# A block table that is worked out earlier: attention and a routed expert layer in one kernel

## The chip, the cores and the metric

The kernel runs on one core of a Trainium2 chip. The metric is the device time of one execution in microseconds (us); for the kernel before, the median of 3 runs is 975.67 us (975.44 to 978.47).

## The reference, cut to what matters

64 attention heads of 576 tokens and 64 dimensions (8 batches of 8 heads), with scores far below the row's largest left out, and then a layer of 8 experts in which each of the 4608 tokens goes to the one expert with the largest logit:

```python
scores = scale * q @ k.T                       # per head, 576 x 576
attn   = softmax(scores where scores >= max(scores) - tau)
x      = (attn @ v) laid out as 4608 x 512     # the 8 heads of a token side by side
logits = x @ w_gate                            # 4608 x 8
for e in range(8):                             # expert_idx = argmax(logits)
    xe = x[expert_idx == e]
    out[expert_idx == e] = gate_w * (relu(xe @ w1[e]) @ w2[e])
```

## The kernel before, in words

The attention half works on 32 pairs of heads, four pairs to a batch `b`. A counter `k` of steps runs through it, 11 steps to a pair. In each step the program emits one tile of scores (`s`, for the row maxima, ahead of the rest by 21 steps), one tile of transposed scores (`st`), its exponential and mask, the casts `ph` and `pl` of the result, and some of the products with v (`av`). All else is hung on steps: `plan(k, f)` and `after(d, f)` have `f` emitted in step `k` or `d` steps from now, at the front, the middle or the end of a step.

Emission order is not yet queue order. When the program is complete, a planner walks a simulated time line and fills each engine's queue: of the instructions that it reckons ready, the one emitted first goes first. An instruction whose inputs and buffers are there early can so be placed far ahead of its step. Each queue then runs strictly in its order, and so do the DMA issues on the queues of SP, ACT and POOL.

When the four pairs of a batch are through, `finish(b)` (L510) normalizes the batch's tokens and writes them into the rows `R`; SP transposes them (`xTg`, L552); `logits(b)` (L560) multiplies with the gate; `route(b)` (L585) finds each token's expert. Nine steps after `route` for batch 5, `ranks` (L616) counts with matmuls (`rk`) which place every token has in its expert's list, writes the places to `posi` (L630), and `send(j)` (L643) lets POOL scatter five tiles of rows to `xs` in DRAM, in steps 6, 8, 10, 12 and 14 after the ranks.

Behind the last scatters of the batches 5, 6 and 7 comes a block table each: `tables0`, `tables1`, `tables2` (L1047 to L1062, named in the dictionary `TABLES`, L1100). `level` calls `counts` (L672: one matmul into a PSUM tile `pc`) and `table_first` (L679): a chain of 11 small VectorE operations and one ScalarE copy, most of them on `pc` itself, that ends in the integer tables `badi` and `row` (both by L669). From `row`, `fetch(m)` (L830) lets POOL gather 128 rows of block `m` out of `xs` (`Rm`, L858); the gather waits for the scatters of the batches placed so far. SP transposes the rows (`xTm`, L868), VectorE and POOL copy their weights and numbers (`gt`, L871 and L876). From step 336 on the products with the experts' weights (`gemm1`, L913, and `gemm2`, L946) run beside the last attention steps, and after step 352 alone.

PSUM: the tiles `pst`, `lg`, `rk` and `pc` share one buffer, the pool `ps_m` with a single bank, so one of them is there at a time. `pst` (L381) is a pair's row maxima, transposed on TensorE; four small operations (L386 to L389) turn them into three rows `ptT`, and three DMAs of SP (L394) put these into the operand `CQ`, which the pair's `st` matmuls (L407) read. The steps are: ranks of batch 5 in step 311, `pst` of pair 30 in 320, `pst` of pair 31 in 331, logits of batch 6 in 335.

Between these steps, too, the first expert's weights are brought in, eight pieces through two buffers `wf`: SP loads a piece (L802), ScalarE casts it (`wb`, L817), TensorE copies the cast to PSUM (`hi_w`, L254), VectorE takes the difference (L255) and frees the buffer.

Of the kernel before, what the change touches and what calls it, by code (L numbers as in the profile page):

```python
# [18 lines left out]
B, H, S, D = 8, 8, 576, 64  # L19
# [31 lines left out]
def kernel(  # L51
# [123 lines left out]
    def plan(k, f, where=END):  # L175
        if urgent[0]:
            f = hurry(f)
        assert (k, where) >= (now[0], slot[0])
        acts.setdefault(k, ([], [], []))[where].append(f)
# [11 lines left out]
    def after(k, f, where=END):  # L191
        plan(now[0] + k, f, where)
# [392 lines left out]
    def route(b, n, dist, Lj, w, got):  # L585

        bc = [P, n, E]

        def t3(nm, dt=F32):
            return small.tile([P, 5, E], dt, tag=nm, name=f"{nm}_{b}", bufs=2)[:, 0:n, :]  # L590

        def t2(nm, dt=F32):
            return small.tile([P, 5, 1], dt, tag=nm, name=f"{nm}_{b}", bufs=2)[:, 0:n, :]

        tt = nc.vector.tensor_tensor
        mx, mw, oh, ex, sm = t2("mx"), t2("mw"), t3("oh", F16), t3("ex"), t2("sm")
        was = small.tile([P, E], F16, tag="was", name=f"was_{b}", bufs=2)
        posi = small.tile([P, 5], I32, tag="posi", name=f"posi_{b}", bufs=2)
        R = rows_of(b)
        Rf = R.bitcast(F32)  # L600
        chain(0, [
            lambda: nc.vector.tensor_reduce(mx, Lj, axis=AX.X, op=ALU.max),
            lambda: tt(w, Lj, mx.to_broadcast(bc), ALU.is_equal),
            lambda: tt(ex, Lj, mx.to_broadcast(bc), ALU.subtract),
            lambda: tt(w, w, rank8.unsqueeze(1).to_broadcast(bc), ALU.mult),
            lambda: nc.vector.tensor_reduce(mw, w, axis=AX.X, op=ALU.max),
            lambda: tt(oh, w, mw.to_broadcast(bc), ALU.is_equal),
            lambda: nc.scalar.copy(was, run),
            lambda: nc.vector.tensor_reduce(got, oh.rearrange("p j e -> p e j"), axis=AX.X, op=ALU.add),
            lambda: nc.scalar.copy(  # L610
                R[:, 0:n, DM + 1:DM + 2], tid[:, b // 2, 4 * (b % 2):4 * (b % 2) + n].unsqueeze(2)
            ),
            lambda: tt(run, run, got, ALU.add),
        ], b == B - 1)

        def ranks(dist=dist):  # L616
            nc.scalar.activation(ex, ex, AF.Exp, scale=1.0 / (SX * SG))
            rk = ps_m.tile([P, 512], F32, tag="m", name=f"rk_{b}")
            rkv = rk[:, 0:n * E].rearrange("p (j e) -> p j e", e=E)
            for j in range(n):  # L620
                nc.tensor.matmul(rkv[:, j], before, oh[:, j], start=True, stop=False)
                for i in range(j):
                    nc.tensor.matmul(rkv[:, j], ones, oh[:, i], start=False, stop=False)
                nc.tensor.matmul(rkv[:, j], ones, was, start=False, stop=True)
            ps = rk[:, 64:64 + n * E].rearrange("p (j e) -> p j e", e=E)
            total = rk[:, 136:136 + n].unsqueeze(2)
            after(1, lambda: tt(ps, rkv, oh, ALU.mult), FRONT)
            def places():
                with nc.allow_low_precision(reason="one whole number below 2^24 among zeros"):
                    nc.vector.tensor_reduce(posi[:, 0:n].unsqueeze(2), ps, axis=AX.X, op=ALU.add)  # L630

            fs = [
                lambda: nc.vector.tensor_reduce(total, ex, axis=AX.X, op=ALU.add),
                lambda: nc.scalar.activation(sm, total, AF.Copy, bias=1e-9),
                places,
                lambda: nc.vector.reciprocal(sm, sm),
                lambda: nc.scalar.activation(Rf[:, 0:n, DM:DM + 1], sm, AF.Copy, scale=1.0 / (SX * SW * SW)),
            ]
            if b == 0:
                fs.append(lambda: nc.vector.tensor_copy(pos0, posi[:, 0:1]))  # L640
            chain(1, fs, b == B - 1)

            def send(j):  # L643
                put = nc.gpsimd.indirect_dma_start(
                    xs[:, :], bass.IndirectOffsetOnAxis(ap=posi[:, j:j + 1].bitcast(U32), axis=0), R[:, j, :], None
                )
                if b < B - 1:
                    tc.keep_in_program_order(put)
                put = put.ins
                tc.declare_no_dep(put, group="puts", reason="each token has a row of its own")  # L650
                tc.declare_no_dep(put, group="gets", reason="gathered rows are those of tokens placed earlier")
                tc.add_to_no_dep_group("puts", put)
                puts.append((b, put))
                sent.add((b, j))

            wait = 1 if b == B - 1 else 6
            if b == B - 1:
                dist = 0
            for j in range(n):
                after(wait + dist * j, lambda j=j: send(j))  # L660
            if b in TABLES:
                after(wait + dist * n, TABLES[b])

        after(0 if b == B - 1 else RK[b], ranks)


# [160 lines left out]
    def late(m):  # L827
        return m == "x" or m >= NEARLY

    def fetch(m):  # L830

        idx, bad, par = slots[m]
        g, i = group_of[m] if m != "x" else ((m,), 0)
        if m in range(NF, NF + 2):

            if "spare" not in T:
                T["spare"] = xp.tile([P, 2, NT * H * W // 2], F32, tag="x", name="spare")
            Rm = T["spare"][:, m - NF, 0:ROW].bitcast(I32)
            xT = T["spare"][:, m - NF, 520:1032].bitcast(F16).rearrange("p (i c t) -> p i c t", i=1, c=8)
        elif m in range(EARLY_SLOTS):  # L840
            Rm = pools[0].tile([P, ROW], I32, tag="Rm", name=f"Rm_{m}", bufs=2)
            xT = pools[0].tile([P, 1, 8, P], F16, tag="xTm", name=f"xTm_{m}", bufs=NF)
        else:
            Rm = R[:, 0 if m == "x" else m % 5]
            if i == 0:
                xT = rpool.tile([P, 2, 8, P], F16, tag="xT", name=f"xTm_{m}", bufs=3)
            else:
                xT = ms[g]["xT"]
        if i == 0:
            ms[g] = dict(xT=xT, par=par, gw=[], ti=[])  # L850
        d = ms[g]
        for z in range(1 + late(m)):
            dst = xT[:, i]
            if late(m):
                Rm = R[:, z if m == "x" else (2 * m + z) % 5]
                dst = xT.rearrange("p i c t -> p (i c t)")[:, 0:8 * PL].rearrange("p (c t) -> p c t", c=8)
                d["xT"], dst = dst, dst[:, :, P * z:P + P2 * z]
            get = nc.gpsimd.indirect_dma_start(  # L858
                Rm, None, xs[:, :], bass.IndirectOffsetOnAxis(ap=idx[:, z:z + 1].bitcast(U32), axis=0)
            )  # L860
            get = get.ins
            mine = [put for b, put in puts if b <= placed.get(m, B - 1)]
            for put in mine:
                tc.add_manual_dep(get, put.name, sync, reason="rows of the tokens placed so far")
            if m != "x":
                tc.declare_no_dep(get, group="puts", keep=mine, reason="rows of tokens placed later are others")
                tc.add_to_no_dep_group("gets", get)
            nc.sync.dma_start_transpose(dst, Rm[0:P2 if z else P, 0:DM].bitcast(F16))  # L868
            gt = small.tile([P, 2], I32, tag="gt", name=f"gt_{m}_{z}", bufs=6)
            gw, ti = gt.bitcast(F32)[:, 0:1], gt[:, 1:2]  # L870
            nc.vector.tensor_copy(gw, Rm.bitcast(F32)[:, DM:DM + 1])  # L871
            to = Rm[:, DM + 1:DM + 2]
            if z:
                nc.gpsimd.tensor_tensor(ti, to, to, ALU.add)
                to = ti
            nc.gpsimd.tensor_tensor(ti, to, bad[:, z:z + 1], ALU.add)  # L876
            d["gw"].append(gw)
            d["ti"].append(ti)
# [168 lines left out]
    def tables0():  # L1047
        T[0] = level("0", ((), EARLY[0]), None)
        for m in range(NF):
            after(1 + m, lambda m=m: fetch(m))  # L1050

    def tables1():
        T[1] = level("1", EARLY, T[0])
# [46 lines left out]
    TABLES = {B - 3: tables0, B - 2: tables1, B - 1: tables2}  # L1100
# [5 lines left out]
    wait = []  # L1106
# [64 lines left out]
    if True:  # L1171
# [18 lines left out]
        while busy:  # L1190
# [3 lines left out]
            for z in (("st", "s"), ("s", "st"))[TUNE["ord"]]:  # L1194
                n, t = divmod(k + (NSTEP + LEAD if z == "s" else 0), NSTEP)
# [11 lines left out]
            n, t = divmod(k - TUNE["av"], NSTEP)  # L1207
# [95 lines left out]
```

## Time and profile before

| what | value |
|---|---|
| median of 3 runs | 975.67 us |
| the profiled execution | 985.67 us, span 983.8 us |
| PE busy | 940.2 us (96%) |
| DVE busy | 696.7 us (71%) |
| ACT busy | 652.0 us (66%) |
| POOL busy | 555.4 us (56%) |
| granted TensorE clock, mean | 0.990 |

PE is TensorE's matmuls, PEld its weight loads, DVE VectorE, ACT ScalarE, POOL GpSimd; a q behind a name is the engine's own instruction queue, with its DMA issues. A time line row has the start, the duration, the line, out<-in, and in brackets how long the engine stood idle before and what ended it. `x2` behind a row means two such instructions merged into one row. Attention alone fills the span up to some 550 us; both halves share it until 563.5 us, where the last `st` matmul stands; after it the experts run alone.

### The profile page before, as it was taken

To read this page: it belongs to the slowest core of one execution; us is meant where nothing else is said; L and a number is where in the kernel's file an instruction comes from. 1 tells how busy PE (TensorE), PEld (TensorE's weight loads), DVE (VectorE), ACT (ScalarE), POOL (GpSimd) and SP (SyncE) were. 2 spreads that over 40 slices of the span, in tenths; PEclk is the share of its full clock that TensorE was granted. 3 is DMA by queue.
4 is the path that set the end of the run, shared out by engine and by line. 5 is a ranking of instruction groups with operands and counts; after the bars stand their busy time and mean duration, and the time that the engine had idled before them with its cause. 6 is when DMAs were issued, how large, how long until landed. Compare 5 with 4: busy or idle time off the path is not lost. (4 is left out here: it accounts for less than half of the span.)

```text
span 983.8 us, 28575 instructions
## 1 busy us (share of the span) xinstructions
PE 940.2 (96%) x11548; PEld 604.5 (61%) x11548; DVE 696.7 (71%) x1413; ACT 652.0 (66%) x1111; POOL 555.4 (56%) x467
## 2 busy tenths in 40 slices
PE   7899999999999999999997989999999999999997
PEld 2355556556566566555564676677667766677684
DVE  8899999999999999999889755735143342433560
ACT  2789898989988989989788844434243342433651
POOL 5466886997978988879879743331212221221121
PEclk9999999999999999999999999999999999999999
DMA  7643455474645664645647469987574556556630
GB/s 199 186 133 77 137 135 146 92 197 115 162 121 166 153 165 107 175 129 119 141 132 196 92 157 306 383 210 190 156 242 123 198 162 170 182 150 217 214 107 28
DMA packets 142707, 159.19 MB, mean 162 GB/s; under 512 B 96361, under 2 KB 112747, under 8 KB 142572
## 3 DMA queue, kind: packets, MB, share of 16 engines
q1 hardware_dynamic: 125782, 100.03, 40.2%
q10 hardware_dynamic: 7638, 27.85, 9.2%
q0 software_dynamic: 9152, 29.45, 8.7%
q8 instruction: 92, 1.51, 0.6%
q14 instruction: 43, 0.35, 0.1%
HBM read 90.24 MB, written 19.44 MB: 111 GB/s over the span
## 5 line engine op out<-in xcount | busy, mean ns | idle before, releaser
L432 POOL TENSOR_TENSOR pl<-e,ph 128x1024 f16<-128x1024 f32 x158 | 336.0, 2137 | 95.2 <-ACT ph L431 56.2
L423 ACT ACTIVATE e<-st,ntau 128x512 f32<-128x512 f32 (+1 forms) x352 | 222.0, 652 | 52.9 <-PE st L407 40.8
L426 DVE SCALAR_TENSOR_TENSOR e<-st,e 128x512 f32<-128x512 f32 (+1 forms) x352 | 219.4, 636 | 12.6 <-ACT e L423 12.0
L946 PE MATMUL y<-wb,hl 128*128 128x512 f16 (+1 forms) x1056 | 203.5, 362 | 0.5 <-ACT xh L491 0.4
L913 PEld LDWEIGHTS <-wb 128*128 128x128 f16 x2304 | 188.3, 98 | 24.6 <-issue 5.2
L913 PE MATMUL h<-xTm,wb 128*128 128x256 f16 (+2 forms) x2112 | 196.3, 253 | 3.0 <-issue 2.5
L370 DVE TENSOR_REDUCE nm<-s 128x1 f32<-128x512 f32 x300 | 188.3, 632 | 14.2 <-PE s L360 12.6
L476 PE MATMUL av<-vop,ph 128*128 128x65 f16 (+3 forms) x3072 | 188.9, 195 | 1.7 <-ACT x L486 1.2
L476 PEld LDWEIGHTS <-ph 128*128 128x128 f16 (+1 forms) x3072 | 158.7, 100 | 47.1 <-issue 17.5
L431 ACT CAST ph<-e 128x1024 f16<-128x1024 f32 x160 | 166.6, 1042 | 5.2 <-DVE e L426 4.6
L476 PE MATMUL av<-vop,pl 128*128 128x65 f16 (+1 forms) x1536 | 168.0, 194 | 1.3 <-POOL pl L432 0.7
L476 PEld LDWEIGHTS <-pl 128*128 128x128 f16 (+1 forms) x1536 | 136.2, 100 | 32.4 <-issue 9.9
L946 PEld LDWEIGHTS <-hl 128*128 128x128 f16 (+1 forms) x1056 | 94.5, 100 | 100.0 <-issue 5.0
L407 PE MATMUL st<-CQ,ck 128*128 128x512 f16 (+3 forms) x640 | 137.4, 289 | 4.1 <-DMA CQ<-ptT 4.1
L825 DVE SCALAR_TENSOR_TENSOR wb<-wf,wb 128x1024 f16<-128x1024 f32 x88 | 103.9, 1221 | 52.4 <-ACT wb L817 50.5
L406 PE MATMUL st<-QK 128*128 128x512 f16 (+3 forms) x640 | 138.9, 294 | 1.5 <-DVE e L426 0.6
L358 PE MATMUL s<-QK 128*128 128x512 f16 (+1 forms) x600 | 129.0, 292 | 1.0 <-DVE nm L370 0.3
L960 POOL DMA_INDIRECT out_dram<-o,gt x40 | 44.8, 1119 | 145.7 <-ACT o L957 129.4
L360 PE MATMUL s<-ck,CQ 128*128 128x512 f16 (+1 forms) x600 | 126.9, 287 | 0.0
L901 ACT ACTIVATE hl<-h 128x512 f16<-128x512 f32 (+1 forms) x80 | 45.8, 573 | 111.7 <-PE h L913 103.0
L817 ACT ACTIVATE wb<-wf 128x1024 f16<-128x1024 f32 x96 | 97.5, 1049 | 30.8 <-DMA wf<-in_w_dram 16.0
L957 ACT ACTIVATE o<-y,gt 128x512 f32<-128x512 f32 (+1 forms) x40 | 26.6, 664 | 93.7 <-PE y L946 76.6
(193 smaller groups left out, 981.6 us busy)
## 6 DMA issues: line engine op xcount, KB each, us to landing
wf<-in_w_dram SPq DMA_DIRECT2D x96, 512.0 KB
qkf<-in_qk_dram ACTq DMA_DIRECT2D x29, 576.0 KB
vf<-in_v_dram ACTq DMA_DIRECT2D x15, 640.0 KB
QK<-hi SPq DMA_DIRECT2D x62, 144.0 KB
QK<-lo SPq DMA_DIRECT2D x62, 72.0 KB
QK<-hi SPq DMA_DIRECT2D x62, 72.0 KB
ck<-lo SPq DMA_DIRECT2D x62, 72.0 KB
CQ<-hi SPq DMA_DIRECT2D x62, 64.0 KB
```

The source lines that it names most:

```text
L358: nc.tensor.matmul(sc[rows, oc], d["QA"][a][:, cols], d["KB"][a][:, CH[c]], start=True, stop=False)
L360: nc.tensor.matmul(sc[rows, oc], d["CQ"][:, at:at + cols.stop - cols.start], d["CK"][a][:, CH[c]], start=False, stop=True,)
L370: nc.vector.tensor_reduce(o, sc[:, 0:width(t)], axis=AX.X, op=ALU.max, negate=True)
L406: nc.tensor.matmul(sc[rows, oc], d["KB"][a][:, cols], d["QA"][a][:, CH[c]], start=True, stop=False)
L407: nc.tensor.matmul(sc[rows, oc], d["CK"][a][:, cols], d["CQ"][:, q], start=False, stop=True)
L423: nc.scalar.activation(pf, sc, AF.Exp, bias=ntau, scale=0.125 / SS)
L426: nc.vector.scalar_tensor_tensor(pf, sc, 0.0, pf, ALU.is_ge, ALU.mult)
L431: nc.scalar.copy(h, pd)
L432: (nc.vector if (n, t) in PLV else nc.gpsimd).tensor_tensor(l, pd, h, ALU.subtract)
L476: nc.tensor.matmul(av[:, 0:D] if z == 2 else av, l if z == 1 else h, vop[:, tv, W:W + D] if z == 2 else vop[:, tv, 0:W], start=i in (0, NT ...
L913: nc.tensor.matmul(o, Wt[:, c, wh, f], x, start=c == 0 and z == 0, stop=c == 3 and z == 2,)
L946: nc.tensor.matmul(o, h[:, hh], Wt[:, f, wh, c], start=f == 0 and z == 0, stop=f == 7 and z == 2)
```

## The change

In `ranks`, the table of batch 5 is emitted 5 steps after the ranks and not 6 + 2 x 5 = 16 steps after them. `tables0` has its three fetches 12, 13 and 14 steps after itself and not 1, 2 and 3, so that they are emitted in the steps 328 to 330 as before. The two other tables are as they were.

```diff
@@ -659,7 +659,7 @@
             if b in TABLES:
-                after(wait + dist * n, TABLES[b])
+                after(5 if b == B - 3 else wait + dist * n, TABLES[b])
@@ -1047,7 +1047,7 @@
     def tables0():
         T[0] = level("0", ((), EARLY[0]), None)
         for m in range(NF):
-            after(1 + m, lambda m=m: fetch(m))
+            after(12 + m, lambda m=m: fetch(m))
```

The table's step so goes from 327 to 316: ahead of the five scatters (steps 317 to 325) and of `pst` of pair 30 (step 320).

## Rows read from the trace of the kernel before

**Rows 1.** The page, busy times: engine, busy us, share of the span, instructions.
```profile
PE 940.2 (96%) x11548; PEld 604.5 (61%) x11548; DVE 696.7 (71%) x1413; ACT 652.0 (66%) x1111; POOL 555.4 (56%) x467
```
**Rows 2.** Stretches: us, length, busy of PE PEld DVE ACT POOL, clock, DMA share, GB/s.
```profile
509.00:521.00 12.00, 10.59 (x149) 5.97 (x150) 9.50 (x22) 11.26 (x23) 9.74 (x8) 1.00 0.53 176
510.00:550.00 40.00, 32.52 (x484) 19.33 (x481) 32.36 (x72) 34.23 (x62) 35.20 (x27) 0.96 0.64 178
535.00:539.00 4.00, 3.59 (x35) 1.92 (x35) 2.83 (x8) 3.65 (x7) 3.81 (x3) 0.58 0.45 139
```
**Rows 3.** Waits of PE from 480 to 640 us: total us, times, longest.
```profile
PE hi_w L254 <- ACT wb L817: 3.9, 3, 2.0
```
**Rows 4.** Time line of PE.
```profile
514.05 0.27 PE L381 MATMUL pst<-ident,r 128*9 128x128 f32 x1
...
530.65 0.59 PE L254 MATMUL hi_w<-wb,ident_h 128*128 128x512 f16 x2 [1.50 <-ACT wb L817]
...
532.89 0.38 PE L407 MATMUL st<-CQ,ck 128*128 128x512 f16 x1
...
535.41 1.01 PE L254 MATMUL hi_w<-wb,ident_h 128*128 128x512 f16 x2 [1.96 <-ACT wb L817]
...
541.77 0.28 PE L381 MATMUL pst<-ident,r 128*9 128x128 f32 x1
...
551.49 0.38 PE L407 MATMUL st<-CQ,ck 128*128 128x512 f16 x1
...
552.75 1.07 PE L913 MATMUL h<-xTm,wb 128*128 128x128 f16 x16 [0.45 <-DMA xTm<-Rm]
```
**Rows 5.** Line 685: duration ns min/median/max, first and last start.
```profile
L685 DVE CAST rk_f<-rk_i x1: 172/172/172, 18.1 to 18.1; 128x32 f32<-128x32 int32 x1
```
**Rows 6.** Instructions on tile pc alone, 523 to 542 us: busy of PE DVE ACT.
```profile
523.00:542.00 19.00, 0.17 (x1) 2.10 (x11) 0.18 (x1) 0.91 0.80 214
```
**Rows 7.** Time line of DVE, first table and what stands around it.
```profile
508.93 0.18 DVE L630 TENSOR_REDUCE posi<-rk 128x5 int32<-128x40 f32 x1
...
522.77 0.27 DVE L389 TENSOR_TENSOR ptT<-pst,ptT 9x128 f16<-9x128 f32 x1
...
523.69 0.14 DVE L676 TENSOR_TENSOR cnt<-pc,base_e 128x8 f32<-128x8 f32 x1
...
541.53 0.19 DVE L669 CAST row<-pc 128x32 int32<-128x32 f32 x1
```
**Rows 8.** Time line of DVE, first and last operation of the second table.
```profile
569.48 0.17 DVE L676 TENSOR_TENSOR cnt<-pc,base_e 128x8 f32<-128x8 f32 x1 [2.42 <-PE pc L674]
...
573.15 0.19 DVE L669 CAST row<-pc 128x32 int32<-128x32 f32 x1
```
**Rows 9.** Time line of ACT.
```profile
516.42 0.36 ACT L386 ACTIVATE ptT<-pst,thr 9x128 f16<-9x128 f32 x1 [0.27 <-PE st L407]
...
575.33 0.20 ACT L610 COPY R<-tid 128x5 int32<-128x5 int32 x1 [0.95 <-DMA xs<-R,posi]
```
**Rows 10.** DMA issues on the queue of SP, in order of time.
```profile
520.87 2.89 SPq L394 DMA_DIRECT2D CQ<-ptT  x2
...
542.53 6.16 SPq L394 DMA_DIRECT2D CQ<-ptT  x3
548.74 1.26 SPq L868 DMA_TRANSPOSE xTm<-Rm  x1
```
**Rows 11.** Time line of POOL.
```profile
529.08 0.99 POOL L644 DMA_INDIRECT xs<-R,posi  x1 [0.17 <-issue]
...
532.37 4.21 POOL L432 TENSOR_TENSOR pl<-e,ph 128x1024 f16<-128x1024 f32 x2
...
544.04 1.01 POOL L858 DMA_INDIRECT Rm<-xs,row  x1 [0.15 <-DVE vop L255]
...
572.29 0.99 POOL L644 DMA_INDIRECT xs<-R,posi  x1 [0.17 <-issue]
```
**Rows 12.** Waits of SP's queue from 480 to 600 us.
```profile
SPq L868 <- DMA Rm<-xs,row: 4.7, 1, 4.7
```

## The prediction

> **What bounds the kernel now.** The busy times of the page come first: PE is busy 940.2 of 983.8 us [rows 1], so a change elsewhere counts only where it lengthens or shortens an idle stretch of PE. The busy times by stretch show where the change falls: from 510 to 550 us PE is busy 32.52 of 40 us [rows 2], so 7.5 us are idle there, the most that a better order can win besides the clock. The waits of PE name their cause: 3.9 us in three waits for ScalarE's cast of a weight piece [rows 3], the two longest 1.50 and 1.96 us, at 530.65 and 535.41 us [rows 4]. After the second one the matmuls are slower (two of 512 columns take 1.01 us, after the first wait 0.59) [rows 4]; the granted clock from 535 to 539 us is 0.58 on the mean [rows 2], between its levels of 1.2 and 2.4 GHz, which costs 0.42 x 4 = 1.7 us. The table itself comes from the time lines: it has the bank of `pst` from 523.7 us (its first VectorE operation) to 541.7 us (the end of `row`), 18.0 us [rows 7], for 11 VectorE operations of 2.10 us, one of ScalarE of 0.18 and a matmul of 0.17 [rows 6]. No wait of PE there is for the table or for a `pst` that it kept out. One row more says how much a step is worth: the table's constant, which the program emits in step 327, was converted at 18.1 us [rows 5]. The planner takes what is ready; a step is a rank, not a time.
>
> **Part by part, in the profiled execution's time.**
>
> *The table's operations* are moved, none is added. The bank is free from 509.1 us on, when `posi` of the ranks is written [rows 7], and step 316 comes about then, so I put its start at 509 to 511 us. Its 2.10 us on VectorE then fall into 509 to 521 us, where VectorE is busy 9.50 of 12 us [rows 2] and so has 2.5 us free: 0. Without that cover they cost at most their 2.1 us; from 523 to 542 us they leave 2.1 us free, at best a gain of as much.
>
> *How long the table keeps the bank.* Between 4.1 us (the second table, from 569.48 us to the end of its `row` at 573.34 us, plus 0.2 for its matmul) [rows 8] and 18.0 us [rows 7]: its end lies between 513.2 and 527.1 us. At step 316 its links are older than nearly all else that is ready, so it is nearer to the second table; with one large VectorE operation slipped into each gap, 11 x (0.19 + 0.68) = 9.6 us. I take its end at 515 to 519 us.
>
> *`pst` of pair 30* is now behind the table, a new wait. It is on PE at 514.05 us [rows 4], so it comes 1 to 5 us later. Behind it stand ScalarE's operation at 516.42 us [rows 9], VectorE's last at 522.77 us [rows 7], and SP's last row DMAs, issued until 520.87 + 2.89 = 523.8 us [rows 10]. The four small operations sum to about 1.2 us; from 514.3 to 523.0 us they have 8.7. So a `pst` 5 us late can still be done by 523 us. The first reader is the matmul at 532.89 us [rows 4], 9.1 us behind the last issue. Cost 0. At the other end (table until 527.1 us, 13 us late) the issues end at 536.8 us, a landing of 2.05 us (a scatter issued until 573.28 us is waited for until 575.33 [rows 9, 11]) makes it 538.9 us, and PE waits 6.0 us.
>
> *`pst` of pair 31* loses its wait: it ran at 541.77 us, right behind `row` [rows 4, 7]. It can come up to 3.6 us earlier, and the logits of batch 6 behind it. Its reader at 551.49 us does not wait [rows 4], though SP's last issue ends only at 542.53 + 6.16 = 548.7 us [rows 10]. Gain 0, but a spare of 2.8 - 2.05 = 0.75 us gets wider.
>
> *Gathers, `xTm`, `gt`.* Their steps are kept, their time is not: they were held up to 544.04 us [rows 11] by `row`. Now the last scatter decides, issued until 530.07 us and landed 2.05 us later at 532.1 us; then POOL has two `pl` until 536.6 us [rows 11]. So two gathers come some 7.5 us earlier, on POOL ahead of later `pl`, which shift by 2 x 1.3 us and win that back where the gathers stood: 0 (uncovered 2.6). Their transposes move up on SP, in front of the rows of pair 31, perhaps: 0 in the forecast, a rival below. The first expert matmul waited 0.45 us for `xTm` [rows 4]; that goes: -0.45. The next input in question is the weight piece, which is there before.
>
> *The fetches' distance and ScalarE's copy* move 0.
>
> Sum: -0.45 us on 985.67 us. That execution is 10.0 us above the median of 975.67 us; I carry the difference over to the median: 975.2 us. About 0.3% (2.9 us) is what a measurement here can tell from no change, so this is no change.
>
> **The rivals.**
>
> A, faster: the weight pieces get through sooner. The table's links stand between VectorE's differences that free `wf`, in a stretch in which PE waits for the pieces [rows 3]. If their 2.1 us leave that loop, half of the 3.9 us of waits goes (1.95), the stretch of lower clock goes with it (1.7), and the 0.45 above: -4.1 us, 971.6 us. For it: PE idles 7.5 us there [rows 2]. Against it: the last step before the waits is a DMA and a cast, and a link takes only 0.19 us of VectorE.
>
> B, slower: SP's queue. The transposes of the blocks come to stand ahead of SP's three row DMAs of pair 31 and hold them while they wait for the gather; such a wait is 4.7 us in this trace [rows 12]. The last row then is issued at 548.7 + 4.7 = 553.4 and landed at 555.4 us, and the matmul at 551.49 us waits 3.9 us. Of the two longest waits for weights one was followed by the low clock [rows 4], so half of 1.7 us comes on top: +4.8 us, 980.4 us. It decides from a delay of 0.75 us on, the spare worked out above. For it: steps 328 to 330 rank ahead of 334, that of the rows; in the kernel before the three transposes begin at 548.74 us, right behind the rows [rows 10]. Against it: the planner counts a gather's landing before it takes its transpose, and `pst` of pair 31 has moved up as well.
>
> The trace so shows the low clock after one of two waits. The Trainium skill, "TensorE: Matmul & The Clock Gate", section "HAM oscillation — how this bites in real kernels", describes it as paid at every wait for a DMA between short bursts. By that rule B has the whole 1.7 us and ends at 3.9 + 1.7 = 5.6, at 981.3 us; the trace disagrees at 530.65 us, and I keep the half.
>
> C, the change does not do what it says: the planner starts the table late again, behind `pst` of pair 30, since it goes by readiness. Then all stays, 975.7 us. Against it: `pc` ranks ahead of this `pst` now, and the bank is free before the pair's maxima are there.
>
> **How the numbers follow.** Forecast 0.47, C 0.05, A 0.27, B 0.21. A's size is at the bound of 2.9 us if only its waits or only its clock come, so a fifth of it falls within; what the new order does to the rest of the queues can push the forecast out on either side, a little over 0.1 together. So faster 0.28, within 0.3% 0.49, slower 0.23. The range goes from A with a little more (970.5) to B with the whole clock term (981.0); the forecast's own is 973 to 978. The 6.0 us of the late `pst` lie just outside.
>
> **What would show it.** Right: in the changed kernel's time line the first table lies between 509 and 520 us; `pst` of pair 30 comes up to 5 us later and its reader does not wait; `pst` of pair 31 stands nearer to 538 than 541.8 us; the first gathers stand at 535 to 538 us; PE is idle 7 to 8 us from 510 to 550 us as before. A shows in fewer waits for `wb` and a clock near 1.00 there; B in a wait of the `st` matmul for `CQ` or a longer one for `wb`, with transposes of blocks ahead of them on SP. The prediction is wrong if the time leaves 973 to 978 us, or if the gathers stay at 544 us.

## The result, and the profile after

The changed kernel takes 986.21 us (median of 5 runs, 982.63 to 987.09), the kernel before in the same set 975.98 us (975.44 to 978.47): a ratio of 1.0082, 95% interval 1.0063 to 1.0100. It is slower by 0.8%, where no change was forecast. Every ratio to the kernel before leaves out slow runs (one only, of the kernel before in the last set, at 999.23 us) and is not the quotient of two medians, which would be 1.0105 here. The level of the kernel before differs between the sets that follow, and drifts within them (medians from 978.11 to 990.27 us), so times are compared within a set.

The profiled execution of the changed kernel is the shortest of its five, 982.63 us with a span of 980.9 us, and that of the kernel before was 10 us above its median: the two traces can't be subtracted as they are. The changed one is 4.2 us ahead already when `posi` is written (504.71 against 508.93 us), before either table begins, so I count from there where times of the two are compared. From `posi` to the last `st` matmul (L407) it needs 57.2 us, the kernel before 54.6, and 55.0 in a second trace. So the first trace shows where time is lost, but only 2.2 to 2.6 us of it. Traces of the changed kernel in the second and fourth set need 63.1 and 61.3 us there; none of the kernel before was taken beside them. The stretch to look at is the one in which the table now lies. Busy times (length, busy of PE, PEld, DVE, ACT, POOL, then clock, DMA share, GB/s) that answer to [rows 2]:

```profile
510.00:550.00 40.00, 29.85 (x412) 17.36 (x410) 30.73 (x71) 31.29 (x55) 33.81 (x29) 0.87 0.72 179
...
520.00:525.00 5.00, 1.91 (x19) 1.25 (x19) 1.91 (x4) 2.67 (x10) 4.81 (x5) 0.52 0.16 58
525.00:530.00 5.00, 4.98 (x21) 1.99 (x20) 4.07 (x8) 3.39 (x5) 4.17 (x5) 0.79 1.06 221
```

PE is idle 10.2 of these 40 us, not 7.5, and its clock is 0.87, not 0.96. The worst five microseconds of the forty begin at 520 us: PE and DVE are busy 1.9 of 5 us each, ACT 2.7. Where three engines idle at once they may be waiting for each other in a row, and the time lines tell in which order. PE's, with the copies of weight pieces 3, 4, 5 and 7 (compare [rows 4]):

```profile
519.57 0.28 PE L381 MATMUL pst<-ident,r 128*9 128x128 f32 x1 [1.35 <-DVE row L669]
523.09 1.01 PE L254 MATMUL hi_w<-wb,ident_h 128*128 128x512 f16 x2 [3.25 <-ACT wb L817]
527.47 0.59 PE L254 MATMUL hi_w<-wb,ident_h 128*128 128x512 f16 x2
532.29 0.59 PE L254 MATMUL hi_w<-wb,ident_h 128*128 128x512 f16 x2 [2.31 <-DVE nm L370]
...
537.59 0.27 PE L381 MATMUL pst<-ident,r 128*9 128x128 f32 x1
540.72 1.01 PE L254 MATMUL hi_w<-wb,ident_h 128*128 128x512 f16 x2 [2.36 <-ACT wb L817]
...
589.12 0.48 PE L570 MATMUL lg<-wg,xTg 128*128 128x8 f16 x12 [3.47 <-DMA xTg<-R]
```

PE stands at `pst` of pair 30 until the table's `row` is written, and right behind it, 3.25 us more, at the copy of the third weight piece. The table (compare [rows 7]; it has the bank from its matmul at 506.3 us) and ScalarE around `pst` (compare [rows 9]):

```profile
504.71 0.18 DVE L630 TENSOR_REDUCE posi<-rk 128x5 int32<-128x40 f32 x1
...
507.41 0.16 DVE L676 TENSOR_TENSOR cnt<-pc,base_e 128x8 f32<-128x8 f32 x1
...
519.32 0.19 DVE L669 CAST row<-pc 128x32 int32<-128x32 f32 x1
521.45 0.35 DVE L387 SCALAR_TENSOR_TENSOR pst<-pst,thr,ptT 9x128 f32<-9x128 f32 x1 [1.94 <-ACT ptT L386]
```
```profile
519.12 1.06 ACT L817 ACTIVATE wb<-wf 128x1024 f16<-128x1024 f32 x1
...
521.06 0.36 ACT L386 ACTIVATE ptT<-pst,thr 9x128 f16<-9x128 f32 x1
521.83 0.25 ACT L388 CAST ptT<-pst 9x128 f16<-9x128 f32 x1 [0.41 <-DVE pst L387]
521.99 1.05 ACT L817 ACTIVATE wb<-wf 128x1024 f16<-128x1024 f32 x1
```

The copy at 523.09 us starts 0.05 us behind the end of the cast at 521.99 us. That cast had no wait for its data (no bracket names a DMA); it stood behind L388, the third small operation on `pst`. So the row is: `row`, `pst` on PE, L386, L387, L388, the cast, the copy. SP stands still too. Its queue (compare [rows 10]):

```profile
504.30 10.66 SPq L802 DMA_DIRECT2D wf<-in_w_dram  x4
521.44 2.29 SPq L394 DMA_DIRECT2D CQ<-ptT  x3
523.78 3.60 SPq L552 DMA_TRANSPOSE xTg<-R  x2
527.51 3.34 SPq L802 DMA_DIRECT2D wf<-in_w_dram  x2
...
537.30 1.23 SPq L868 DMA_TRANSPOSE xTm<-Rm  x1
...
543.33 2.32 SPq L394 DMA_DIRECT2D CQ<-ptT  x3
```

From 514.96 to 521.44 us it issues nothing; the rows of pair 30 stand at its head, and the load of the fifth weight piece behind them. That load needs a buffer which only the late third copy frees, so SP's standstill need not cost anything by itself; the third set tries it. The first gathers (compare [rows 11]) did come earlier, 27.7 us behind the start of `posi` and not 35.1, and nothing shows for it:

```profile
532.39 1.01 POOL L858 DMA_INDIRECT Rm<-xs,row  x1 [0.15 <-issue]
533.70 0.96 POOL L858 DMA_INDIRECT Rm<-xs,row  x1 [0.30 <-issue]
```

What the copy waits for stands in the code, not in the profile. `split_w`, which casts the weight pieces, has these lines in both kernels:

```python
817        hi = nc.scalar.activation(o[:, :, 0], x, AF.Copy, scale=SW)
818        if e == 0:
819            tc.keep_in_program_order(hi)
```

Line 819 ties a cast behind the ScalarE instruction that the program emitted last before it. By the steps in the code that is L388 of pair 30 for the third piece, before and after the change. In the queue of ScalarE, as the planner fills it, the pieces (counted from 1) and the operations of `pst` stand so:

```
before:   1  2  L386  L388  3  4      on PE: pst, copies 1 2 3 4
changed:  1  2  4  L386  L388  3      on PE: copies 1 2, pst, copies 3 4
```

In the kernel before the tie held nothing, as `pst` was early: L388 was done 1.8 us ahead of the third cast, and other work of ScalarE lay between.

```profile
519.55 0.25 ACT L388 CAST ptT<-pst 9x128 f16<-9x128 f32 x1
...
521.63 1.03 ACT L817 ACTIVATE wb<-wf 128x1024 f16<-128x1024 f32 x1
```

With `pst` behind the table it holds the third cast, and with it the loop of two weight buffers. That it is the tie and not some other reason is inferred here; the third set tests it.

### The profile page after: what moved, and what is told of

Same layout as the page of the kernel before. It is cut to its first block, busy times and chain, and to the rows that moved or that the text cites. A ratio compares the mean times of both kernels' runs of the same rounds, so it can differ in the third digit from the quotient of the medians.

```text
span 980.9 us, 28574 instructions
## 1 busy us (share of the span) xinstructions
PE 935.2 (95%) x11548; PEld 606.2 (62%) x11548; DVE 696.0 (71%) x1413; ACT 651.9 (66%) x1111; POOL 558.4 (57%) x467
## 5 line engine op out<-in xcount | busy, mean ns | idle before, releaser
L913 PEld LDWEIGHTS <-wb 128*128 128x128 f16 x2304 | 190.7, 99 | 18.8 <-DMA wf<-in_w_dram 0.2
L476 PEld LDWEIGHTS <-pl 128*128 128x128 f16 (+1 forms) x1536 | 135.7, 100 | 35.1 <-issue 9.8
L407 PE MATMUL st<-CQ,ck 128*128 128x512 f16 (+3 forms) x640 | 137.7, 289 | 4.7 <-DMA CQ<-ptT 3.9
L871 DVE COPY gt<-R 128x1 f32<-128x1 f32 x33 | 5.1, 153 | 132.0 <-DMA out_dram<-o,gt 105.6
```

The lines of the kernel that those rows point to most:

```text
L407: nc.tensor.matmul(sc[rows, oc], d["CK"][a][:, cols], d["CQ"][:, q], start=False, stop=True)
L476: nc.tensor.matmul(av[:, 0:D] if z == 2 else av, l if z == 1 else h, vop[:, tv, W:W + D] if z == 2 else vop[:, tv, 0:W], start=i in (0, NT ...
L913: nc.tensor.matmul(o, Wt[:, c, wh, f], x, start=c == 0 and z == 0, stop=c == 3 and z == 2,)
```

## Experiments

Each is a change of the kernel named, and each was timed in five rounds beside the kernel before.

**First set: bank or queue.** Theory "bank" says that the one PSUM bank, which the table now has ahead of `pst`, makes the cost; theory "SP", my rival B, that it is the early gathers' transposes on SP; theory "late", that it is the last batch's transposes, mixed with those of spare blocks on SP (the wait of 3.47 us at 589.12 us above). The unchanged kernel shows what the set can tell apart.

> The kernel before, unchanged: a second trace and the spread of its own time. The profiled execution of the kernel before lay 10 us over its median while that of the changed kernel lay 4 us under its own, so the two traces can't be subtracted as they are. Every theory: 975.5 to 978.5 us, ratio 1.000 within 0.002, and a trace whose stretch up to the ranks of batch 5 is some 4 us shorter than in the first one.

986.11 us (12 runs, 983.49 to 997.04), ratio 1.000 [0.997, 1.003]. The level is 10 us above the one I had expected, and the trace reaches `posi` 1.9 us earlier than the first (507.08 us), not 4.

Early table in the shared bank, gathers held back behind the POOL work that stood ahead of them before:

```diff
 861: -get = get.ins
      +get = (tc.keep_in_program_order(get) if m in range(NF) else get).ins
1050: -after(12 + m, lambda m=m: fetch(m))
      +after((18, 18, 23)[m], lambda m=m: fetch(m))
```

> The changed kernel, but its three gathers are pinned behind the POOL work that stands ahead of them in the kernel before (emitted 18, 18 and 23 steps after the table, and kept in program order). The table still has the bank ahead of pst of pair 30; the transposes of the blocks stand behind the rows of pair 31 on SP again. Theory bank (the late pst, in front of which PE waits, and the row DMAs and weight pieces held behind it): about as slow as the changed kernel, 984 to 987 us. Theory SP (transposes of blocks ahead of weight loads on SP's queue): back to 975 to 978 us. Theory late (the transposes of batch 7 mixed with those of the spare blocks on SP, a wait of 3.5 us and low clock from 585 to 597 us): back too, since that order is that of the kernel before.

993.18 us, ratio 1.0061 [1.0035, 1.0088]. The gathers are late (the first on POOL at 551.00 us, 41.1 us behind `posi` and so later than in the kernel before, 35.1), and the cost is there, with the same two stops of PE. Some of it may be the edit's own: the first expert matmul waits 1.85 us for `xTm`.

```profile
525.98 0.28 PE L381 MATMUL pst<-ident,r 128*9 128x128 f32 x1 [1.69 <-DVE row L669]
529.60 1.01 PE L254 MATMUL hi_w<-wb,ident_h 128*128 128x512 f16 x2 [3.34 <-ACT wb L817]
```

The changed kernel, the first table in a bank of the scores' pool; and the same with the gathers held back:

```diff
 673: -pc = ps_m.tile([P, 512], F32, tag="m", name=f"pc_{nm}")
      +pc = (ps_sc if nm == "0" else ps_m).tile([P, 512], F32, tag="sc" if nm == "0" else "m", ...
```

> The changed kernel, but the first table's pc takes one of the six buffers of the scores for its time, and not the bank that pst uses. pst of pair 30 then no longer waits; the gathers come as early as in the changed kernel. Theory bank: back to 975 to 978 us. Theory SP: as slow as the changed kernel, 984 to 987 us, with a wait for a weight piece behind a transpose. Theory late: slower by 3 to 5 us, 979 to 982 us, since the order of the spare blocks and batch 7 on SP is again mixed.

984.34 us, ratio 0.9963 [0.9936, 0.9990]. The table is as early (`cnt` at 507.48 us), `pst` runs at 512.72 us without waiting, the third copy at 522.14 us without waiting.

> Both at once: the table early in a scores buffer, the gathers pinned late. Theory bank and theory SP: 975 to 978 us. Theory late: 979 to 982 us, since batch 7 and the spare blocks are mixed on SP here too.

982.79 us, ratio 0.9959 [0.9937, 0.9982]. Theory SP falls: early gathers cost nothing where the table has its own bank, and holding them back left a cost of 0.6% where it has not. Theory late falls as the main cause: it expected the kernel with its own bank to stay 3 to 5 us slow. The cost is tied to the shared bank.

**Second set: what is it about the late `pst`?** Theory "queue" says that the weight pieces pay, which stand behind the waiting `pst` and its small operations; theory "rows", that its rows come late to their readers. First the changed kernel again, against the thought that the first ratio was the chip's:

> The changed kernel again, now in turns with the kernel before on one chip: in the first set the kernel before took 986.8 us on this chip and not 975.7, so the 10 us of the first comparison may in part be one of chips. Theory bank: slower by what the traces show from the ranks of batch 5 to the last attention product, where the changed kernel needs 73.3 us, the kernel before 71.1 and 72.2, and the one with pinned gathers (slower by 0.6%) 76.6: some +2 to +5 us, ratio 1.002 to 1.005. Theory chip (there is no difference, it was all between chips): ratio 1.000 within 0.002.

995.47 us, ratio 1.0087 [1.0054, 1.0121]. It is the kernel, and it costs more than the 1.002 to 1.005 that I had read off the traces.

The changed kernel with `pst` of pair 30 emitted three steps later, so that it no longer stands ahead of the third piece:

```diff
 398: -(after if n >= 1 else lambda k, f: hurry(f)())(1, turn)
      +(after if n >= 1 else lambda k, f: hurry(f)())(4 if n == 30 else 1, turn)
```

> The changed kernel, but pst of pair 30 is emitted 4 steps later than its pair asks for (step 323, not 320). The table still has the bank first. In the queues the weight casts now stand ahead of the small operations on pst on ScalarE, and a weight load ahead of the three row DMAs on SP. Theory queue (it is not the lateness of the rows that costs, but what stands behind the waiting pst in the queues of PE, ScalarE and SP): the waits of 1.35 us for row and 3.25 us for the cast before the third weight piece go, and the low clock after them; ratio to before 0.996 to 1.000. Theory rows (pair 30's rows come too late for its first st matmul): slower than the changed kernel, ratio 1.005 or more, with a wait of st for CQ.

993.93 us, ratio 1.0088 [1.0057, 1.0118]: nothing recovered, against what theory queue expected of it; nor does a `st` matmul wait for `CQ`, as theory rows had it. The trace says why. The third copy is free, but PE still reaches `pst` before the table is done, now the fourth piece's cast stands behind L386 (ScalarE's time line), and the eighth piece's copy waits 3.89 us:

```profile
523.03 0.60 PE L254 MATMUL hi_w<-wb,ident_h 128*128 128x512 f16 x2
526.92 0.38 PE L381 MATMUL pst<-ident,r 128*9 128x128 f32 x1 [2.13 <-DVE row L669]
...
550.69 1.01 PE L254 MATMUL hi_w<-wb,ident_h 128*128 128x512 f16 x2 [3.89 <-ACT wb L817]
```
```profile
528.05 0.36 ACT L386 ACTIVATE ptT<-pst,thr 9x128 f16<-9x128 f32 x1
528.94 1.04 ACT L817 ACTIVATE wb<-wf 128x1024 f16<-128x1024 f32 x1
529.89 0.24 ACT L388 CAST ptT<-pst 9x128 f16<-9x128 f32 x1
```

The kernel before with its late table in the scores' pool:

> The kernel before (table emitted in step 327, fetches right behind it), but with the first table in a scores buffer. Whether the 0.4% that the early table in such a buffer wins over the kernel before is from the bank or from the early table. Theory bank: pst of pair 31 is free of the table here too, so ratio 0.996 to 0.998 as there. Theory early: the earlier table is what wins, so ratio 1.000 within 0.002.

984.20 us, ratio 0.9985 [0.9963, 1.0006]. It tells little: a late table in its own bank is about as good as in the shared one, and the interval holds the early table in its own bank (0.9963) as well.

**Third set: the order edge.** Line 819 found, theory "edge" says that its tie of the third cast makes most of the cost. The kernel to tell it apart takes the edge away for that one piece. No run takes it out of the kernel before, so what the edit does there is not shown.

```diff
 819: -tc.keep_in_program_order(hi)
      +tc.keep_in_program_order(hi) if (w, c) != (0, 2) else None
```

> The changed kernel, but ScalarE's cast of the third weight piece is not held behind the ScalarE instruction that the program emits just before it (in the changed kernel that is the third small operation on pst of pair 30, L388). The table stays early in the shared bank, and pst of pair 30 still waits behind it; the gathers stay early. Theory 'edge': the cost is that this order edge carries the third piece, and with it the whole loop of two weight buffers, behind pst and so behind the table. Then it goes: ratio to the kernel before 0.995 to 1.002, the third hi_w within 1.5 us behind the end of its own cast and before 524 us, longest wait for wb under 2.5 us. Rival 'bank': the lateness of pst of pair 30 itself costs (its rows come late to the st matmuls, PE stops at it for row). pst comes at least as late here, so the ratio stays at 1.005 or above, with a wait of PE at pst or at an st matmul for CQ of over 1.5 us.

981.96 us, ratio 1.0036 [1.0016, 1.0056]: more than half of the 1.0082 and 1.0087 of the earlier sets is gone, though not down to the 1.002 I expected; the rival's 1.005 was not reached either. The third cast now stands ahead of L386 (518.95 against 524.73 us), so it was the tie that held it. The planner, free of the edge, puts `pst` behind the third and fourth copies:

```profile
520.04 0.59 PE L254 MATMUL hi_w<-wb,ident_h 128*128 128x512 f16 x2 [1.47 <-ACT wb L817]
522.56 0.77 PE L254 MATMUL hi_w<-wb,ident_h 128*128 128x512 f16 x2
523.78 0.27 PE L381 MATMUL pst<-ident,r 128*9 128x128 f32 x1
```

`pst` is late as ever, but PE has work until the table is done and does not stop at it. So the edit takes away two things, the tied cast and PE's stop at `pst`, and its price is that of both.

The two ScalarE operations of `pst` of pair 30 moved to VectorE, so that the edge leads elsewhere:

```diff
 386: +lambda: v.tensor_scalar(t[:, 0], x, thr[0:9], None, ALU.add) if n == 30 else a.activation(...
 388: +lambda: v.tensor_copy(t[:, 1], y) if n == 30 else a.copy(t[:, 1], y),
```

> The changed kernel, but the two operations of pst of pair 30 that run on ScalarE (L386, L388) run on VectorE. The order edge of the third weight cast then leads to an older ScalarE instruction and no longer to pst; bank, table and gathers stay as in the changed kernel. Theory 'edge': ratio 0.995 to 1.003, no wait over 2.5 us for wb in the first four pieces. Rival 'bank': 1.005 or above, as pst still comes behind the table. If cast_free recovers and this one does not, the two small operations cost VectorE more than the edge cost PE, which I hold for unlikely (0.6 us).

983.63 us, ratio 1.0054 [1.0036, 1.0073]: a miss. The first four pieces run as expected (third copy at 520.87 us after a wait of 1.14 us, no stop at `pst`), but the late rows are felt later, at the first readers of `CQ` and a piece behind them:

```profile
539.22 1.44 PE L407 MATMUL st<-CQ,ck 128*128 128x512 f16 x3 [1.48 <-DMA CQ<-ptT]
542.75 1.01 PE L254 MATMUL hi_w<-wb,ident_h 128*128 128x512 f16 x2 [2.09 <-ACT wb L817]
```

The edge is therefore not the only way in which a late `pst` costs time. How much of this is the edit's own doing is open: on VectorE the four small operations take from `pst` at 524.60 us to 534.52 us, 9.9 us, where the changed kernel needs 2.8 and the one without the edge 8.0. The rows of pair 30 issued on ScalarE's queue, the edge kept:

```diff
 393: -(nc.sync if n >= 1 else nc.scalar).dma_start(
      +(nc.sync if n >= 1 and n != 30 else nc.scalar).dma_start(
```

> The changed kernel, but the three row DMAs of pair 30 are issued from ScalarE's queue and not from SP's. SP's loads of the weight pieces five to eight no longer stand behind rows that wait for pst; the order edge of the third cast stays. Theory 'edge': little is won, ratio 1.005 to 1.011, the wait of the third hi_w for wb of 3 us or more stays. Rival 'SP': the cost is the loads that stand behind the late rows; then the fifth piece's load comes 3 us or more earlier against the end of pst, the later waits for wb go, and the ratio falls to 1.003 or below.

983.89 us, ratio 1.0069 [1.0044, 1.0094], as theory edge had it: the fifth piece's load comes at 525.07 us (527.51 in the changed kernel's first trace), 2.0 us earlier behind `pst` where rival SP asked for 3, and the third copy still waits 3.72 us. The late rows at the head of SP's queue are not what costs most.

**Fourth set: side by side.** The changed kernel, without the edge, without the edge and with the gathers held back, and with the table in its own bank, all on one chip.

> The changed kernel once more, as the measure for the three others on the same chip. Theory 'edge': 1.007 to 1.011, with the third hi_w 3 us or more behind pst. Rival 'bank' expects the same.

> The changed kernel without the order edge of the third weight cast, beside the changed kernel itself. Theory 'edge', now with a rest for the late pst: 1.002 to 1.005, 3 to 7 us under the changed kernel. If the earlier ratio of 1.0036 was drift of the chip, it comes within 2 us of the changed kernel.

> The changed kernel without the order edge of the third weight cast, and with the three gathers held back to where they were before. It tells what the rest of 0.36% is. If the early gathers and their transposes are the rest, the ratio is 0.997 to 1.0015. If the late pst of pair 30 (rows, the pieces five to seven behind it) is the rest, it stays at 1.002 to 1.006.

> The changed kernel with the first table in a bank of the scores' pool, so that pst of pair 30 does not wait for it; the order edge stays and, since pst is early, holds nothing back. Both theories: 0.993 to 0.999, below the kernel with the edge gone; the distance to that one is the price of the late pst by itself.

| kernel | median, range (us) | ratio to before | start of `posi` to the last `st` matmul, traced (us) |
|---|---|---|---|
| changed | 995.33, 989.80 to 997.26 | 1.0054 [1.0029, 1.0079] | 61.3 (507.88 to 569.13) |
| no edge | 988.56, 987.06 to 993.35 | 0.9990 [0.9963, 1.0017] | 54.0 (506.48 to 560.49) |
| no edge, gathers held back | 991.53, 989.11 to 993.77 | 1.0009 [0.9985, 1.0034] | 58.3 (508.38 to 566.68) |
| own bank | 983.24, 980.47 to 985.97 | 0.9927 [0.9898, 0.9956] | 52.2 (507.18 to 559.41) |

The kernel before wandered from 983.05 to 996.41 us in this set (median 990.27), and the ratios are lower than in the sets ahead. The first, second and fourth so miss what I wrote (1.007 to 1.011, 1.002 to 1.005 and 0.993 to 0.999); the distances between the four are the better measure. Without the edge the changed kernel is 6.8 us faster, as theory edge had it (3 to 7 us), a ratio of medians of 0.9932 [0.992, 0.996] (95%, resampled from the 12, 12 and 11 runs). From there to the own bank it is 5.3 us more, 0.9946 [0.993, 0.997]. The kernel with the gathers held back has a ratio that I had written down for early gathers as the rest (0.997 to 1.0015), but that range rested on the earlier level; beside its neighbour it is 3.0 us slower. Early gathers are so not seen to cost anything, but this kernel can't price them by itself, for it pays for late ones:

```profile
555.38 1.46 PE L913 MATMUL h<-xTm,wb 128*128 128x128 f16 x12 [3.34 <-DMA xTm<-Rm]
```

The stretch from 510 to 550 us, in this order without the third:

```profile
510.00:550.00 40.00, 26.92 (x336) 15.36 (x334) 28.60 (x66) 29.91 (x54) 33.24 (x27) 0.86 0.76 180
```
```profile
510.00:550.00 40.00, 32.94 (x488) 19.99 (x487) 33.01 (x76) 34.66 (x60) 35.90 (x31) 0.96 0.73 188
```
```profile
510.00:550.00 40.00, 33.69 (x505) 20.91 (x504) 34.83 (x81) 36.80 (x65) 37.91 (x32) 0.96 0.77 195
```

Without the edge PE is busy 6.0 us more in the same stretch, at a clock of 0.96 and not 0.86, and it is through with the last `st` matmul 7.2 us sooner behind `posi`: nearly the whole distance of 6.8 us is found here. Between the second and the third there is only 0.75 us of PE's time, and 1.8 us up to the last `st` matmul. The rest of their distance comes later. From 580 to 600 us, where the last batch's logits wait for their transposes, the granted clock differs:

```profile
580.00:600.00 20.00, 16.19 (x195) 12.41 (x194) 9.26 (x18) 5.85 (x8) 3.26 (x6) 0.83 1.12 250
```
```profile
580.00:600.00 20.00, 16.16 (x262) 12.98 (x260) 8.33 (x18) 6.86 (x10) 2.23 (x3) 1.00 1.13 281
```

The own bank has 1.00 there, the kernel without the edge 0.83, which is at most 0.17 x 20 = 3.4 us of full speed, an estimate. Why the last transposes come less well there I could not settle; the queues of SP differ in that place as a whole. So the 5.3 us between no edge and the own bank stay unexplained in the main.

## Why the prediction was wrong

**The table's place and time** look better than they are. It starts at 506.3 us (said: 509 to 511) and has the bank until 519.5 us (said: 515 to 519), in a trace that is 4.2 us ahead. Counted from the start of `posi`, the start at 1.6 us is as forecast (0 to 2), but the end at 14.8 us is not (6 to 10); that the plain numbers nearly agree is luck. The table keeps the bank 13.2 us and not some 9.6: its operations stand in VectorE's queue between more large ones than the one per gap that I had allowed.

**The step that failed is `pst` of pair 30, "Cost 0".** It came 5.5 us later than in [rows 4] by the clock of the traces, but 9.7 us later counted from `posi` (said: 1 to 5), and in the last set 11.5 us later, so counted, than in the kernel with its own bank (524.02 against 511.80 us). The working priced one thing only, the reader of its rows at the end of the chain, and found 9.1 us of room there. That part held: in the changed kernel no `st` matmul waits for `CQ`. What it left out is everything that stands behind a waiting instruction in a queue that runs in order: PE's own next instructions behind `pst`, and ScalarE's third cast, tied behind L388 by line 819. Together 1.35 + 3.25 = 4.6 us of idle PE in one place, a low clock after it, and a weight loop that comes late from there on (in the last set the eighth piece's copy at 551.27 us with the edge, at 542.15 without; 1.4 us of that lie ahead of `posi`). By the experiments the shared bank costs 12.1 us against an own one. Of these, 6.8 go with the edge, PE's stop at `pst` included; for the other 5.3 the mechanism is open. The text did say that "the new order" might push the forecast out, "a little over 0.1 together", without a mechanism or a price.

**Later `pst`, as the other end.** The table until 527 us and a late reader, 6.0 us, were put just outside the range. The sign was right and the size near (8 us by the ratio, 10.2 by the medians), but by luck: PE lost the time at the weight pieces, not at the rows.

**`pst` of pair 31** stands at 537.59 us (said: nearer to 538 than 541.8), but that is the trace's lead again: behind `posi` it comes at 32.9 us, in the kernel before at 32.8. It did not move up; in the kernel with its own bank (last set) it stands at 30.3. **The gathers** came at 532.39 and 533.70 us (said: 535 to 538), and counted from `posi` 7.4 us earlier, as forecast (7.5); that they cost nothing fits the first set. The one term of the sum, the first expert matmul's wait of 0.45 us for `xTm`, is gone as forecast.

**Rival B** named the right sign, with a time of 980.4 us against 986.21, by a wrong mechanism: `xTm` did move ahead of the rows of pair 31 on SP (537.30 against 543.33 us), but no `st` matmul waited for `CQ`, and holding the gathers back left the cost. (The end of the stated range, 981.0 us, is also 0.3 below the 981.3 that the text works out for this rival with the whole clock term.) **Rival A**, fewer waits for `wb`, went the other way: 5.6 us in two waits where [rows 3] have 3.9 in three. What speaks for its idea is the own bank, which is faster than the kernel before in both sets; the reason is not shown. **Rival C** did not come about.

**The clock.** Of the changed kernel's three waits of over 2 us in front of a weight copy, 3.25 and 2.36 us were followed by slow copies (1.01 us for two) and 2.31 us was not (0.59 us): two of three, where the prediction had taken the half. The Trainium skill, "TensorE: Matmul & The Clock Gate", section "HAM oscillation — how this bites in real kernels", tells of waits for a DMA of some 3 to 5 us between short bursts, each with a dip behind it. Only the first of these three waits is of that length, and for it the trace agrees. The 1.50 us at 530.65 us in [rows 4], which the prediction held against the page, is shorter than what the page tells of and so does not contradict it; but the dips behind 2.36 us here, and 1.96 us there, came after shorter waits too.

## What to carry to other kernels

An instruction that is moved behind a shared buffer must be priced by what stands behind it on every in-order queue that it touches, and not by its last reader's slack. Look for order edges that are written by hand: one that costs nothing while its anchor is early becomes a wait the moment the anchor moves. If a small, long chain of operations needs a bank, give it another than the one in which short, urgent tiles pass through: here the kernel with its own bank had 0.4 and 0.7% less time than the kernel before in its two sets, where the changed one had 0.5 to 0.9% more in its three.

## What was not expected of the hardware

By the medians the same change cost 10.2 us where the kernel before stood at 975.98 us, 9.8 where it stood at 985.69, and 5.1 in the last set, where it stood at 990.27 and itself drifted by 13 us (983.05 to 996.41 us), more than the effect. Only the distances between kernels that ran side by side priced an edge of 6.8 us. And a stop of PE costs more than its length: in the last set's changed kernel PE waited 1.69 us for `row` and 3.34 us for the third cast, up to 527.64 us. The two copies then took 1.01 us and not 0.59, and the granted clock was 0.53 in the stretch of 5 us in which the second wait ended and 0.79 in the one behind it:

```profile
524.02 0.28 PE L381 MATMUL pst<-ident,r 128*9 128x128 f32 x1 [1.69 <-DVE row L669]
527.64 1.01 PE L254 MATMUL hi_w<-wb,ident_h 128*128 128x512 f16 x2 [3.34 <-ACT wb L817]
...
525.00:530.00 5.00, 2.36 (x20) 1.40 (x20) 1.91 (x4) 2.67 (x8) 4.81 (x5) 0.53 0.08 25
530.00:535.00 5.00, 4.75 (x20) 1.90 (x19) 4.51 (x9) 2.97 (x5) 2.83 (x3) 0.79 1.08 185
```
